# Packed loads, four warming products and a second issuing engine at the start of an attention, soft-MoE and gated-product kernel

## The chip, the cores and the metric

The kernel runs on one core of a Trainium2 chip. The metric is the device time of one execution in microseconds; lower is better. Of each run the profile gives, beside the time, the span from the first to the last instruction.

## What is computed

Three stages follow each other. Attention: 4 batches of 12 heads, 448 tokens of 64 numbers each, float32. Queries and keys are divided by their root mean square and multiplied by gains, then come the scaled scores, the softmax and the product with the values. Its output, laid out as 1792 tokens of 768 numbers, goes through a soft mixture of experts (8 experts of 4 slots, hidden width 1024), and that through a gated product.

```python
q_n, k_n = rmsnorm(q, g_q), rmsnorm(k, g_k)
scores = q_n @ k_n.T / sqrt(64)
attn = softmax(scores)
x = (attn @ v) as [1792, 768]
...
logits = x @ phi                      # 768 x 32
slots = softmax(logits, over tokens).T @ x
slot_out[e] = relu(slots[e] @ w1[e]) @ w2[e]
x = softmax(logits, over slots) @ slot_out
...
out = ((x @ w_a) * (x @ w_b)) @ w_out # 768 -> 1536 -> 768
```

## The kernel before

Attention works on 24 pairs of heads. A token row of 448 is cut into 4 chunks of 112 partitions (`NC`, `P`). For each pair `load_qk` brings queries and keys into one of three places in a wide tile (`xw` in the trace; pair p uses place p mod 3, so the load of pair 3 waits until pair 0 has been normalised, and that of pair 4 for pair 1). `square` and `sumsq` make the sums of squares (tiles `sq`, `ssq`), `rsqrt` the inverse roots (`nt`, `rinv`: a logarithm and an exponential on ScalarE, then three small steps on VectorE), `normalise` the normalised pair (tile `n`, one half on VectorE for the first two pairs, else all on GpSimd). `emit_T` transposes it on TensorE (`pst`) and writes four rounded parts into a tile `e`, of which there is one for all pairs but pair 1. `emit_Z` stacks these parts into the two tiles `z` of the pair by six transfers within the on-chip memory, three for each head: 64 rows of 1344, 448 and 896 numbers. All transfers are issued by SyncE, in program order.

The loop `for j in range(NPAIR + 1)` then goes through the pairs in 8 steps each. A step n issues `score(n+2)` (two products on TensorE into `pss`, and the row maximum `nmx` on VectorE), `expo(n+1)` (the exponential `p` on ScalarE, with the maximum as bias), `ptrans(n)` (the transpose of `p`, and its copy `pt`) and in every second step the products with the values. Preparing the pairs to come is spread over the steps: `emit_T` and `emit_Z` of pair j+2 in steps 4 to 6, the squares of pair j+4 on GpSimd in step 1, their sums on VectorE in steps 5 and 7.

Ahead of the loop stands a written-out start: `warm` (products of the identity matrix whose results nobody reads, 22 of them at first and `W1` = 15 just ahead of the first score), loads, `prep` (squares on ScalarE, sums on VectorE), `norm`, `normalise`, `emit_T` and `emit_Z` of pairs 0 and 1, then `prep` and `norm` of pairs 2 and 3, then `score(0)`, `score(1)` and `expo(0)`. The order on TensorE, ScalarE, GpSimd and SyncE is that of the code; on VectorE a scheduler fixes it when the program is built. Every engine works its own list in order, so that an instruction that waits holds up all behind it.

The two later stages stream the weights of the experts and of the gated product from HBM. The printed functions below are those that the change touches.

Of the kernel before, what the change touches and what calls it, by code (L numbers as in the profile page):

```python
# [32 lines left out]
def kernel(  # L33
    ctx: ExitStack,
    tc: tile.TileContext,
    q: bass.AP,
    k: bass.AP,
# [11 lines left out]
    B, H, S, D = q.shape  # L49
    NT, DM = out.shape  # L50
    E, F = w1.shape[0], 1024
    NS = phi.shape[1]
    DF = 128 * len(LAGS)
    NC = 4
    P = S // NC
# [27 lines left out]
    W1 = 15  # L83
# [107 lines left out]
    with ExitStack() as c1:  # L191
# [28 lines left out]
        def load_qk(p):  # L220
            if p >= NPAIR:
                return
            b, hp = divmod(p, HP)
            t = qk_sb[0:P, p % 3 * 1024:(p % 3 + 1) * 1024].rearrange("p (i h x) -> p i h x", i=2, h=2)
            for i, src in enumerate((q, k)):
                sp.dma_start(out=t[:, i], in_=src[b, 2 * hp:2 * hp + 2].rearrange("h (p c) d -> p h (c d)", c=NC))
            qk_t[p] = t

        def load_v(p):
            if p >= NPAIR:  # L230
                return
            b, hp = divmod(p, HP)
            src = v[b, 2 * hp:2 * hp + 2].rearrange("h (p c) d -> p h c d", c=NC)
            if p < NPAIR - 1:
                t = vp.tile([P, 2, NC, D], F32, tag="v", name=f"v{p}")
                sp.dma_start(out=t, in_=src)
                v_t[p] = [t[:, hd] for hd in range(2)]
            else:
                x = tk.tile([128, S], F32, tag="l4", name="v23a", bufs=1)[0:P, 0:NC * D]
                y = tk.tile([P, 4, 2, 32], F32, tag="c2", name="v23b", bufs=1)  # L240
                v_t[p] = x.rearrange("p (c d) -> p c d", d=D), y.rearrange("p c (a e) s -> p c (a e s)", a=2)
                for hd in range(2):
                    sp.dma_start(out=v_t[p][hd], in_=src[:, hd])
# [3 lines left out]
        def square(p, i, eng=None):  # L247
            if p >= NPAIR:
                return
            sq = sqp.tile([P, 512], F32, tag="sq", name="sq")  # L250
            a = qk_t[p][:, i].rearrange("p h x -> p (h x)")
            if eng is act:
                act.activation(out=sq, in_=a, func=AF.Square)
            else:
                pool.tensor_tensor(out=sq, in0=a, in1=a, op=ALU.mult)  # L255
            sq_t[p, i] = sq
# [38 lines left out]
        def normalise(p, eng=None):  # L295
# [3 lines left out]
            n_t[p] = npp.tile([P, 2, NC, 2, D], F32, tag="n", name=f"n{p}")  # L299
            for i in range(2):  # L300
                (eng if eng and i == 0 else pool).tensor_tensor(  # L301
                    out=n_t[p][:, i].rearrange("p c h d -> p h c d"),
                    in0=qk_t[p][:, i].rearrange("p h (c d) -> p h c d", d=D),
                    in1=rinv_t[p][:, i, :].rearrange("p (h c) -> p h c", h=2).unsqueeze(3).to_broadcast(
                        [P, 2, NC, D]
                    ),
                    op=ALU.mult,
# [3 lines left out]
        def emit_T(p, i):  # L311
# [12 lines left out]
            for c in range(NC):  # L324
                pe.transpose(ps[:, c * P:(c + 1) * P], src[:, i, c].rearrange("p h d -> p (h d)"), ident[0:P, 0:P])  # L325
# [10 lines left out]
        def emit_Z(p):  # L336
# [3 lines left out]
            for hd in range(2):  # L340
# [3 lines left out]
                sp.dma_start(out=z[D:128, 0].bitcast(F32), in_=src[:, 3])  # L344
# [214 lines left out]
        for i, g in enumerate((g_q, g_k)):  # L559
            for r in range(2):  # L560
                sp.dma_start(out=g4[r * D:(r + 1) * D, i:i + 1], in_=g.rearrange("(d o) -> d o", o=1))
        dve.scalar_tensor_tensor(
            out=gg, in0=g4[:, 0:1], scalar=float(D) ** 0.5, in1=g4[:, 1:2], op0=ALU.mult, op1=ALU.mult
        )
# [4 lines left out]
        norm(0)  # L569
        prep(1)  # L570
        normalise(0, dve)
# [6 lines left out]
        load_qk(4)  # L578
        prep(2)
        emit_T(1, 0)  # L580
        emit_T(1, 1)
        emit_Z(1)
        warm(ps_s.tile([128, 512], F32, tag="s", name="warm"), W1)
# [600 lines left out]
_INS = ["q", "k", "v", "g_q", "g_k", "moe_phi", "moe_w1", "moe_w2", "moe2_w"]  # L1184
# [38 lines left out]
```

## Time and profile before

| what | value |
|---|---|
| time, median of 3 runs | 591.48 us (590.6 to 592.62) |
| profiled execution | 593.33 us |
| its span | 591.5 us |
| PE busy | 557.4 us (94%) |
| ACT busy | 359.6 us (61%) |
| DVE busy | 349.6 us (59%) |
| mean granted TensorE clock | 0.984 |

The profile names PE for TensorE's products, PEld for its weight loads, DVE for VectorE, ACT for ScalarE, POOL for GpSimd and SPq for SyncE's queue of transfers. A shared time in the chain of work that ended last is the time in which that instruction, and nothing else, held up the end. The start, up to the first score, takes the first 21 us; the attention loop runs to some 340 us.

### The profile page before, as it was taken

To read this page: it belongs to the slowest core of one execution; us is meant where nothing else is said; L and a number is where in the kernel's file an instruction comes from. 1 tells how busy PE (TensorE), PEld (TensorE's weight loads), DVE (VectorE), ACT (ScalarE), POOL (GpSimd) and SP (SyncE) were. 2 spreads that over 40 slices of the span, in tenths; PEclk is the share of its full clock that TensorE was granted. 3 is DMA by queue.
4 is the path that set the end of the run, shared out by engine and by line. 5 is a ranking of instruction groups with operands and counts; after the bars stand their busy time and mean duration, and the time that the engine had idled before them with its cause. 6 is when DMAs were issued, how large, how long until landed. Compare 5 with 4: busy or idle time off the path is not lost.

```text
span 591.5 us, 10977 instructions
## 1 busy us (share of the span) xinstructions
PE 557.4 (94%) x3980; PEld 366.9 (62%) x3980; DVE 349.6 (59%) x703; ACT 359.6 (61%) x845; POOL 114.0 (19%) x136
## 2 busy tenths in 40 slices
PE   5989999999999999999999998898989999999997
PEld 5755555566565665655656554343665656689996
DVE  5877777678787687776767521122228888842210
ACT  4677787787887787877877721111169899432210
POOL 1233433333433333333110000010100000200000
PEclk9899999999999999999999999989989999999999
DMA  7955677788697978697676689999999993002332
GB/s 176 220 142 140 165 175 168 209 235 223 165 261 153 266 178 240 166 271 188 156 216 170 271 330 351 426 395 425 428 423 421 418 406 144 1 28 80 92 94 83
DMA packets 39573, 134.51 MB, mean 227 GB/s; under 512 B 5856, under 2 KB 25312, under 8 KB 33120
## 3 DMA queue, kind: packets, MB, share of 16 engines
q1 hardware_dynamic: 39520, 133.81, 72.0%
q8 instruction: 32, 0.52, 0.4%
q14 instruction: 21, 0.17, 0.1%
HBM read 95.26 MB, written 5.51 MB: 170 GB/s over the span
## 4 chain that ended last, share of the span: by engine, by line
PE 75%; DMA 10%; DVE 4%; ACT 4%; SPq 3%; issue 2%; ACTq 0%; DVEq 0%
PE psv L396 12%; PE pspt L382 11%; PE pss L358 5%; DMA z<-e 5%; PE pss L359 5%; PE psM L938 5%; DMA wu_w<-in_moe_w_dram 5%; PE pso L1138 3%; PE pso L1140 3%; PE pso L1139 3%; PE psS L721 3%; PE psh L697 3%; PE pst L325 3%; PE psS L938 2%; PE psx L509 2%
## 5 line engine op out<-in xcount | busy, mean ns | idle before, releaser
L360 DVE TENSOR_REDUCE nmx<-pss 112x1 f32<-112x448 f32 x192 | 118.4, 619 | 40.9 <-PE pss L359 40.5
L369 ACT ACTIVATE p<-pss,nmx 112x448 f32<-112x448 f32 x192 | 123.7, 644 | 9.2 <-DVE nmx L360 6.3
L382 PEld LDWEIGHTS pspt<-ident,p 112*112 112x112 f32 x768 | 80.4, 133 | 78.9 <-ACT pt L388 27.5
L382 PE MATMUL pspt<-ident,p 112*112 112x112 f32 x768 | 110.0, 266 | 1.5 <-ACT p L369 1.4
L388 ACT COPY pt<-pspt 112x448 f32<-112x448 f32 x144 | 76.9, 534 | 27.1 <-PE pspt L382 25.6
L396 PE MATMUL psv<-pt,v 112*64 112x448 f32 x368 | 90.3, 569 | 0.0
L358 PE MATMUL pss<-z 128*112 128x448 f32 x192 | 85.1, 443 | 0.0
L301 POOL TENSOR_TENSOR n<-xw,rinv 112x512 f32<-112x512 f32 x46 | 47.1, 1043 | 174.7 <-PE pst L325 109.7
L359 PE MATMUL pss<-z 128*112 128x448 f32 x192 | 70.5, 367 | 0.0
L386 DVE COPY pt<-pspt 112x448 f32<-112x448 f32 x48 | 29.9, 623 | 20.9 <-PE pspt L382 20.8
L255 POOL TENSOR_TENSOR sq<-xw 112x512 f32<-112x512 f32 x40 | 40.9, 1041 | 5.4 <-DMA xw<-in_q_dram 4.9
L369 ACT ACTIVATION_READ_ACCUMULATOR p<-pss,nmx 112x1 f32 x192 | 40.0, 208 | 0.0
L1138 PE MATMUL pso<-Mh,t 128*128 128x384 f32 x112 | 37.9, 338 | 0.5 <-DVE Ml L967 0.5
L358 PEld LDWEIGHTS pss<-z 128*112 128x112 f32 x192 | 34.0, 177 | 6.7 <-issue 5.8
L1139 PE MATMUL pso<-Ml,t 128*128 128x384 f32 x112 | 37.7, 337 | 0.0
L1140 PE MATMUL pso<-Mh,t 128*128 128x384 f32 x112 | 37.7, 337 | 0.0
L325 PE MATMUL pst<-ident,n 112*128 112x112 f32 x192 | 27.1, 267 | 10.9 <-ACT rd L427 6.3
L1157 DVE COPY ot<-pso 128x384 f32<-128x384 f32 (+1 forms) x14 | 7.6, 543 | 49.5 <-PE pso L1142 49.5
L396 PEld LDWEIGHTS psv<-pt,v 112*64 112x64 f32 x368 | 18.3, 135 | 29.5 <-issue 22.4
L359 PEld LDWEIGHTS pss<-z 128*112 128x112 f32 x192 | 34.2, 178 | 0.7 <-issue 0.6
L938 PE MATMUL psM<-w,G 128*128 128x512 f32 x64 | 33.8, 610 | 0.8 <-DVE w L818 0.8
L818 DVE SCALAR_TENSOR_TENSOR xw<-wu_w,top 128x768 int32<-128x768 int32 x24 | 22.3, 953 | 19.6 <-ACT top L804 19.6
(177 smaller groups left out, 891.7 us busy)
## 6 DMA issues: line engine op xcount, KB each, us to landing
wu_w<-in_moe_w_dram SPq DMA_DIRECT2D x38, 1536.0 KB, 11.0
z<-e SPq DMA_DIRECT2D x48, 336.0 KB, 4.6
z<-e SPq DMA_DIRECT2D x48, 224.0 KB, 4.4
r<-in_moe_w_dram SPq DMA_DIRECT2D x7, 1536.0 KB, 8.6
xw<-in_moe_w_dram SPq DMA_DIRECT2D x4, 1536.0 KB, 13.7
xw<-in_q_dram SPq DMA_DIRECT2D x24, 224.0 KB, 4.5
xw<-in_k_dram SPq DMA_DIRECT2D x24, 224.0 KB, 4.0
z<-e SPq DMA_DIRECT2D x48, 112.0 KB, 4.4
```

The source lines that it names most:

```text
L301: (eng if eng and i == 0 else pool).tensor_tensor(out=n_t[p][:, i].rearrange("p c h d -> p h c d"), in0=qk_t[p][:, i].rearrange("p h (c d) ...
L358: pe.matmul(ps, x, z[:, 1, :], start=True, stop=False)
L359: pe.matmul(ps, x, z[:, 2, :], start=False, stop=True)
L360: dve.tensor_reduce(out=nm_of[n // 8][:, h % 2, c:c + 1], in_=ps, axis=AX.X, op=ALU.max, negate=True)
L369: act.activation(out=t, in_=ps_of.pop(n), func=AF.Exp, bias=nm_of[n // 8][:, h % 2, c:c + 1], accum_out=den_t[n // 8][:, h % 2, c:c + 1],)
L382: pe.transpose(ps[:, kc * P:(kc + 1) * P], src[:, kc * P:(kc + 1) * P], ident[0:P, 0:P])
L388: act.copy(out=o, in_=i)
L396: pe.matmul(av_t[p][hd * D:(hd + 1) * D, 0:S], v_t[p][hd][:, kc, :], pt_t[2 * p + hd][:, kc, :], start=(kc == 0), stop=(kc == NC - 1),)
L938: pe.matmul(o, G[:, r], W[:, c], start=st, stop=sp_)
L1138: pe.matmul(o, ch[:, m], Mh[:, m, c], start=(m == 0), stop=False)
L1139: pe.matmul(o, ch[:, m], Ml[:, m, c], start=False, stop=False)
L1140: pe.matmul(o, cl[:, m], Mh[:, m, c], start=False, stop=False)
```

## The change

Queries and keys are packed on the host into one array `qk`, whose rows hold both, in the order in which they are normalised, and the values are laid out likewise; one transfer now loads a pair (two for pair 0). `W1` is 4 instead of 15. The middle one of the three transfers of each stack (64 rows of 448) is issued by ScalarE for pairs 0 and 1. `normalise(0)` stands ahead of `prep(1)`, the product of the gains (tile `few`) behind both, and `load_qk(4)` and `prep(2)` behind `emit_Z(1)`.

```diff
--- before.py
+++ after.py
@@ -33,8 +33,7 @@
 def tile_attention_softmoe_gate_kernel(
     ctx: ExitStack,
     tc: tile.TileContext,
-    q: bass.AP,
-    k: bass.AP,
+    qk: bass.AP,
     v: bass.AP,
     g_q: bass.AP,
     g_k: bass.AP,
@@ -46,13 +45,16 @@
 ):
     nc = tc.nc
     pe, act, dve, pool, sp = nc.tensor, nc.scalar, nc.vector, nc.gpsimd, nc.sync
-    B, H, S, D = q.shape
     NT, DM = out.shape
+    D = g_q.shape[0]
+    NC = 4
+    P = qk.shape[1]
+    S = NC * P
+    B = NT // S
+    H = DM // D
     E, F = w1.shape[0], 1024
     NS = phi.shape[1]
     DF = 128 * len(LAGS)
-    NC = 4
-    P = S // NC
     HP = H // 2
     NPAIR = B * HP
     KD = DM // 128
@@ -80,7 +82,7 @@
     W3 = 2
     W4 = 7
     W5 = 3
-    W1 = 15
+    W1 = 4
     DV = 7
     P2_ENGINES = {ET.PE, ET.SP}
 
@@ -220,27 +222,26 @@
         def load_qk(p):
             if p >= NPAIR:
                 return
-            b, hp = divmod(p, HP)
-            t = qk_sb[0:P, p % 3 * 1024:(p % 3 + 1) * 1024].rearrange("p (i h x) -> p i h x", i=2, h=2)
-            for i, src in enumerate((q, k)):
-                sp.dma_start(out=t[:, i], in_=src[b, 2 * hp:2 * hp + 2].rearrange("h (p c) d -> p h (c d)", c=NC))
-            qk_t[p] = t
+            qk_t[p] = qk_sb[0:P, p % 3 * 1024:(p % 3 + 1) * 1024].rearrange("p (i x) -> p i x", i=2)
+            if p == 0:
+                for i in range(2):
+                    sp.dma_start(out=qk_t[p][:, i], in_=qk[p][:, i])
+            else:
+                sp.dma_start(out=qk_t[p], in_=qk[p])
 
         def load_v(p):
             if p >= NPAIR:
                 return
-            b, hp = divmod(p, HP)
-            src = v[b, 2 * hp:2 * hp + 2].rearrange("h (p c) d -> p h c d", c=NC)
             if p < NPAIR - 1:
                 t = vp.tile([P, 2, NC, D], F32, tag="v", name=f"v{p}")
-                sp.dma_start(out=t, in_=src)
+                sp.dma_start(out=t, in_=v[p])
                 v_t[p] = [t[:, hd] for hd in range(2)]
             else:
                 x = tk.tile([128, S], F32, tag="l4", name="v23a", bufs=1)[0:P, 0:NC * D]
                 y = tk.tile([P, 4, 2, 32], F32, tag="c2", name="v23b", bufs=1)
                 v_t[p] = x.rearrange("p (c d) -> p c d", d=D), y.rearrange("p c (a e) s -> p c (a e s)", a=2)
                 for hd in range(2):
-                    sp.dma_start(out=v_t[p][hd], in_=src[:, hd])
+                    sp.dma_start(out=v_t[p][hd], in_=v[p][:, hd])
 
         sq_t = {}
 
@@ -248,7 +249,7 @@
             if p >= NPAIR:
                 return
             sq = sqp.tile([P, 512], F32, tag="sq", name="sq")
-            a = qk_t[p][:, i].rearrange("p h x -> p (h x)")
+            a = qk_t[p][:, i]
             if eng is act:
                 act.activation(out=sq, in_=a, func=AF.Square)
             else:
@@ -296,15 +297,11 @@
             if p >= NPAIR:
                 return
             assert not any(x[0] == p for x in small)
-            n_t[p] = npp.tile([P, 2, NC, 2, D], F32, tag="n", name=f"n{p}")
+            n_t[p] = npp.tile([P, 2, 8, D], F32, tag="n", name=f"n{p}")
             for i in range(2):
                 (eng if eng and i == 0 else pool).tensor_tensor(
-                    out=n_t[p][:, i].rearrange("p c h d -> p h c d"),
-                    in0=qk_t[p][:, i].rearrange("p h (c d) -> p h c d", d=D),
-                    in1=rinv_t[p][:, i, :].rearrange("p (h c) -> p h c", h=2).unsqueeze(3).to_broadcast(
-                        [P, 2, NC, D]
-                    ),
-                    op=ALU.mult,
+                    out=n_t[p][:, i], in0=qk_t[p][:, i].rearrange("p (n d) -> p n d", d=D),
+                    in1=rinv_t[p][:, i].unsqueeze(2).to_broadcast([P, 8, D]), op=ALU.mult,
                 )
             qk_t.pop(p)
 
@@ -322,7 +319,7 @@
             src = n_t[p]
             ps = ps_m.tile([128, 512], F32, tag="m", name="pst")[:, 0:S]
             for c in range(NC):
-                pe.transpose(ps[:, c * P:(c + 1) * P], src[:, i, c].rearrange("p h d -> p (h d)"), ident[0:P, 0:P])
+                pe.transpose(ps[:, c * P:(c + 1) * P], src[:, i, 2 * c:2 * c + 2].rearrange("p h d -> p (h d)"), ident[0:P, 0:P])
             if i == 0:
                 act.activation(out=et[:, 0], in_=ps, func=AF.Copy)
                 dve.tensor_tensor(out=et[:, 3], in0=ps, in1=et[:, 0].bitcast(F32), op=ALU.subtract)
@@ -341,7 +338,7 @@
                 z = zt[(2 * p + hd) % NZ]
                 src = et[hd * D:(hd + 1) * D].bitcast(F32)
                 sp.dma_start(out=z[0:D, 0:3].bitcast(F32), in_=src[:, 0:3])
-                sp.dma_start(out=z[D:128, 0].bitcast(F32), in_=src[:, 3])
+                (act if p < 2 else sp).dma_start(out=z[D:128, 0].bitcast(F32), in_=src[:, 3])
                 sp.dma_start(out=z[D:128, 1:3].bitcast(F32), in_=src[:, 1:3])
 
         def score(n):
@@ -559,27 +556,27 @@
         for i, g in enumerate((g_q, g_k)):
             for r in range(2):
                 sp.dma_start(out=g4[r * D:(r + 1) * D, i:i + 1], in_=g.rearrange("(d o) -> d o", o=1))
-        dve.scalar_tensor_tensor(
-            out=gg, in0=g4[:, 0:1], scalar=float(D) ** 0.5, in1=g4[:, 1:2], op0=ALU.mult, op1=ALU.mult
-        )
         load_qk(2)
         load_v(0)
         sp.dma_start(out=phi_sb, in_=phi.rearrange("(k p) s -> p k s", p=128))
         prep(0)
         norm(0)
+        normalise(0, dve)
+        dve.scalar_tensor_tensor(
+            out=gg, in0=g4[:, 0:1], scalar=float(D) ** 0.5, in1=g4[:, 1:2], op0=ALU.mult, op1=ALU.mult
+        )
         prep(1)
-        normalise(0, dve)
         load_qk(3)
         emit_T(0, 0)
         emit_T(0, 1)
         emit_Z(0)
         norm(1)
         normalise(1, dve)
-        load_qk(4)
-        prep(2)
         emit_T(1, 0)
         emit_T(1, 1)
         emit_Z(1)
+        load_qk(4)
+        prep(2)
         warm(ps_s.tile([128, 512], F32, tag="s", name="warm"), W1)
         norm(2)
         normalise(2)
@@ -1181,7 +1178,7 @@
             split(i + 2)
 
 
-_INS = ["q", "k", "v", "g_q", "g_k", "moe_phi", "moe_w1", "moe_w2", "moe2_w"]
+_INS = ["qk", "v", "g_q", "g_k", "moe_phi", "moe_w1", "moe_w2", "moe2_w"]
 _OUTS = [((1792, 768), "float32")]
 
 
@@ -1205,6 +1202,12 @@
 
     nc = _bacc.Bacc("TRN2", target_bir_lowering=False, num_devices=1)
     arrays, args = {}, []
+    q, k, v = (inputs.pop(x) for x in "qkv")
+    b, h, n, d = q.shape
+    q, k, v = (x.reshape(b, h // 2, 2, n // 4, 4, d) for x in (q, k, v))
+    qk = _np.stack([x.transpose(0, 1, 3, 4, 2, 5) for x in (q, k)], axis=3)
+    inputs["qk"] = qk.reshape(b * h // 2, n // 4, 2, 8 * d)
+    inputs["v"] = v.transpose(0, 1, 3, 2, 4, 5).reshape(b * h // 2, n // 4, 2, 4, d)
     inputs["moe2_w"] = _in_units(*(inputs.pop(f"moe2_w_{x}") for x in ("a", "b", "out")))
     for name in ("moe_w1", "moe_w2"):
         a = inputs[name]
```

The change moves instructions on three engines, all in the start.

ScalarE's list from the first copy of pair 0's transpose on, before (`e_208` and `z_141`, `z_142` are pair 0, `e_248` pair 1; `ssq_198`, `ssq_243`, `ssq_297` are pairs 1, 2 and 3; `p_319` is the first exponential):

```order
L327 ACTIVATE e_208<-pst 128x448
L330 ACTIVATE e_208<-pst,few 128x448
L286 ACTIVATE nt<-ssq_198,few 112x16
L287 ACTIVATE rinv_229<-nt 112x16
L253 ACTIVATE sq<-xw_65 112x512 x2
L327 ACTIVATE e_248<-pst 128x448
L330 ACTIVATE e_248<-pst,few 128x448
L286 ACTIVATE nt<-ssq_243,few 112x16
L287 ACTIVATE rinv_285<-nt 112x16
L253 ACTIVATE sq<-xw_65 112x512 x2
L286 ACTIVATE nt<-ssq_297,few 112x16
L369 ACTIVATE p_319,den<-pss,nmx 112x448
```

ScalarE's list from pair 0's second copy on, in the change (`e_205`, `e_236` are pairs 0 and 1, `ssq_199`, `ssq_260`, `ssq_282` pairs 1, 2 and 3, `p_304` the first exponential):

```order
L327 ACTIVATE e_205<-pst,few 128x448
L341 DMA z_141<-e_205 64x448
L341 DMA z_142<-e_205 64x448
L287 ACTIVATE nt<-ssq_199,few 112x16
L324 ACTIVATE e_236<-pst 128x448
L327 ACTIVATE e_236<-pst,few 128x448
L341 DMA z_143<-e_236 64x448
L341 DMA z_144<-e_236 64x448
L254 ACTIVATE sq<-xw_65 112x512 x2
L287 ACTIVATE nt<-ssq_260,few 112x16
L254 ACTIVATE sq<-xw_65 112x512 x2
L366 ACTIVATE p_304,den<-pss,nmx 112x448
```

Two issues of transfers now stand behind each pair's copies, and the two squares of pair 2 stand behind pair 1's instead of ahead of them.

VectorE's list from the last parts of pair 1 to the fifth row maximum, before (`ssq_412` are the sums of pair 4):

```order
L331 SCALAR_TENSOR_TENSOR e_248<-pst,few,e_248 128x448
L288 SCALAR_TENSOR_TENSOR nt<-rinv_285 112x16
L290 SCALAR_TENSOR_TENSOR nt<-ssq_243,nt 112x16
L263 TENSOR_REDUCE ssq_297<-sq 112x8
...
L292 SCALAR_TENSOR_TENSOR rinv_302<-nt,rinv_302 112x16
L360 TENSOR_REDUCE nmx<-pss 112x1 x3
L263 TENSOR_REDUCE ssq_412<-sq 112x8 x2
L360 TENSOR_REDUCE nmx<-pss 112x1
L386 COPY pt_329<-pspt 112x4x112
L360 TENSOR_REDUCE nmx<-pss 112x1 x4
```

The same stretch of VectorE's list in the change (`ssq_396` are the sums of pair 4):

```order
L328 SCALAR_TENSOR_TENSOR e_236<-pst,few,e_236 128x448
L357 TENSOR_REDUCE nmx<-pss 112x1
L264 TENSOR_REDUCE ssq_260<-sq 112x8 x2
L357 TENSOR_REDUCE nmx<-pss 112x1 x2
...
L293 SCALAR_TENSOR_TENSOR rinv_287<-nt,rinv_287 112x16
L264 TENSOR_REDUCE ssq_396<-sq 112x8
L357 TENSOR_REDUCE nmx<-pss 112x1
L383 COPY pt_313<-pspt 112x4x112
L264 TENSOR_REDUCE ssq_396<-sq 112x8
L357 TENSOR_REDUCE nmx<-pss 112x1 x4
```

The sums of pair 2 have moved behind the first maximum, and a sum of pair 4 stands ahead of the fourth maximum as before, the other now between the fourth and the fifth.

SyncE's list between the load of pair 3 and that of pair 4, before (the load of pair 4 is the two rows of `in_q_dram` and `in_k_dram`):

```order
L345 DMA z_142<-e_208 64x896
L226 DMA xw_65<-in_q_dram 112x2x256
L226 DMA xw_65<-in_k_dram 112x2x256
L343 DMA z_143<-e_248 64x1344
L344 DMA z_143<-e_248 64x448
L345 DMA z_143<-e_248 64x896
```

SyncE's list between the same loads in the change (the last row is the loads of pairs 4 and 5):

```order
L230 DMA xw_65<-in_qk_dram 112x1024
L340 DMA z_141<-e_205 64x1344
L342 DMA z_141<-e_205 64x896
L340 DMA z_142<-e_205 64x1344
L342 DMA z_142<-e_205 64x896
L340 DMA z_143<-e_236 64x1344
L342 DMA z_143<-e_236 64x896
L340 DMA z_144<-e_236 64x1344
L342 DMA z_144<-e_236 64x896
L230 DMA xw_65<-in_qk_dram 112x1024 x2
```

The load of pair 4 stood between the stacks of pairs 0 and 1 and now stands behind both. From there on, and on TensorE and GpSimd apart from the eleven products, the lists are the same but for the packed loads.

## Rows read from the trace of the kernel before

**Rows 1.** Busy time by stretch, with granted clock, DMA share and GB/s.

```profile
21.00:61.00 40.00, 36.46 (x227) 22.70 (x225) 30.66 (x62) 30.60 (x84) 14.63 (x16) 0.96 0.67 155
61.00:340.00 279.00, 271.83 (x1795) 165.38 (x1794) 203.69 (x439) 218.13 (x594) 82.97 (x91) 1.00 0.77 204
395.00:475.00 80.00, 73.12 (x641) 45.12 (x644) 39.52 (x57) 44.02 (x52) 4.83 (x5) 0.96 1.01 421
```

**Rows 2.** The chain that ended last, in order of time: start, us, what.

```profile
16.79 0.68 DVE e L331
...
20.85 0.99 DVE nt L290
...
22.04 1.59 DVE nmx L360 x3
23.64 1.19 DVE ssq L263 x2
24.82 0.54 DVE nmx L360
...
36.94 4.42 DMA z<-e
```

**Rows 3.** Timeline of the start: start, us, engine, instruction, idle before it.

```profile
8.18 0.68 DVE L301 TENSOR_TENSOR n<-xw,rinv 112x512 f32<-112x512 f32 x1
...
10.52 0.31 ACT L286 ACTIVATE nt<-ssq,few 112x16 f32<-112x16 f32 x1
10.68 0.68 DVE L331 SCALAR_TENSOR_TENSOR e<-pst,few,e 128x448 fp32r<-128x448 f32 x1
...
12.62 1.04 POOL L301 TENSOR_TENSOR n<-xw,rinv 112x512 f32<-112x512 f32 x1 [4.38 <-DVE rinv L292]
12.91 1.30 DVE L301 TENSOR_TENSOR n<-xw,rinv 112x512 f32<-112x512 f32 x1
...
14.36 1.72 PE L325 MATMUL pst<-ident,n 112*128 112x112 f32 x8 [4.45 <-DVE n L301]
```

**Rows 4.** Timeline of SyncE's queue: transfers issued.

```profile
11.94 0.59 SPq L344 DMA_DIRECT2D z<-e  x1
...
14.37 1.02 SPq L344 DMA_DIRECT2D z<-e  x1
...
17.72 0.66 SPq L226 DMA_DIRECT2D xw<-in_k_dram  x1
...
32.92 0.47 SPq L343 DMA_DIRECT2D z<-e  x1
```

**Rows 5.** Transfers issued at 17.5 to 18 us: KB, us to landing.

```profile
xw<-in_k_dram SPq DMA_DIRECT2D x1, 224.0 KB, 4.1
```

**Rows 6.** Timeline from the warming products to the loop.

```profile
15.87 5.39 PE L186 MATMUL warm<-ident 128*128 128x128 f32 x30
...
20.76 1.04 POOL L255 TENSOR_TENSOR sq<-xw 112x512 f32<-112x512 f32 x1
...
21.02 0.44 PE L358 MATMUL pss<-z 128*112 128x448 f32 x1
...
22.61 0.64 ACT L369 ACTIVATE p<-pss,nmx 112x448 f32<-112x448 f32 x1 [2.85 <-DVE nmx L360]
...
25.47 0.64 ACT L369 ACTIVATE p<-pss,nmx 112x448 f32<-112x448 f32 x1 [0.29 <-DVE nmx L360]
...
26.51 0.65 ACT L369 ACTIVATE p<-pss,nmx 112x448 f32<-112x448 f32 x1
```

**Rows 7.** Busy time by stretch: the stack of pair 2, and a later stretch.

```profile
34.00:40.50 6.50, 6.50 (x46) 4.14 (x44) 4.43 (x10) 4.02 (x13) 1.24 (x2) 1.00 0.96 213
43.00:47.00 4.00, 4.00 (x17) 1.93 (x16) 2.51 (x6) 2.51 (x8) 2.04 (x2) 0.58 0.28 58
```

**Rows 8.** DMA view, 395 to 470 us: the streamed weights.

```profile
DMA packets 2906, 31.77 MB, mean 424 GB/s; under 512 B 322, under 2 KB 322, under 8 KB 322
```

**Rows 9.** Timeline of ScalarE around pair 3's first copy.

```profile
41.61 0.54 ACT L327 ACTIVATE e<-pst 128x448 fp32r<-128x448 f32 x1 [2.79 <-DMA z<-e]
```

## Prediction, made before the changed kernel ran

> **What bounds the kernel now.** I read the busy time by stretch first. From 61 to 340 us TensorE is busy 271.83 of 279 us, from 395 to 475 us the transfers are busy all the time, at 421 GB/s [rows 1]. Neither stretch is touched by the change but for the packed loads, so what the change is worth is read from the first 61 us, and then it is asked whether a shift there reaches the end. From 21 to 61 us TensorE is idle 3.5 us, and its busy time there includes waits at a lower clock.
>
> Second, the chain that ended last, from 16 to 42 us. The reader is to see that it does not run through the warming products. It goes through the last part of pair 1 (ends 17.47), sums of squares and two small steps of the inverse root on VectorE that are drawn out to about 1 us, the first three row maxima at 22.04, the sums of pair 4 (1.19 us), the fourth maximum at 24.82, then ScalarE's exponentials, and the stack of pair 2 [rows 2]. The warming products end at 21.26 and the first score starts at 21.02, so they release the scores less than 1 us ahead of the moment at which VectorE would have come to a maximum anyway [rows 2, 6]. So the start has two chains of nearly one length: TensorE's, which the change shortens, and that of preparing pairs 2 to 4, whose order it changes.
>
> Third, the timelines of the start for the durations, and SyncE's queue for the order of the transfers.
>
> **The change, part by part.**
>
> *Four products instead of 15.* Fifteen took 5.39 us, 0.36 each; eleven fewer are 3.95 us of TensorE [rows 6]. Beside the other chain this alone is worth at most the few tenths between the third score and the first maximum.
>
> *Pair 0.* VectorE's list now has both sums of pair 1 and the gains ahead of the last step of pair 0's root or of `normalise`. Half of the normalising is VectorE's, and beside GpSimd's half (12.62 to 13.66) it took 1.30 us in pair 1, against 0.68 in pair 0 [rows 3]. I take it that VectorE's half now ends behind GpSimd's, 0.4 us later than before (bounds 0 and 0.9; the packed first load, of which the trace has no row, may give some of it back). The last part of pair 0 then ends at 11.36 + 0.4 = 11.8.
>
> *ScalarE issues transfers.* No row of before shows ScalarE issuing. The nearest are SyncE's issues of the same transfer, 0.59 and 1.02 us [rows 4]; the bounds are 0 and 1.0 each, and I take 0.6. Behind the two issues wait the logarithm of pair 1 (10.52 before), and with it everything of pair 1: it starts at about 11.25 + 1.2 = 12.5. From the logarithm to pair 1's transposes took 10.52 to 14.36, 3.84 us, with two sums of pair 2 in VectorE's way (about 0.65 each), which are now behind; 2.5 us remain, so the transposes start at about 15.0, 0.6 later, less up to 0.6 if the normalising no longer waits for GpSimd. Pair 1's last part ends at 17.7 (16.5 with free issues, 18.7 with dear ones) against 17.47.
>
> *Squares of pair 2 behind pair 1.* Before, they were done while pair 1 waited. Now two issues (1.2), the two squares, two sums, logarithm and exponential, two squares of pair 3, its two sums, and again logarithm and exponential stand between pair 1's copy (ends 17.0) and the first exponential of the loop: about 7 us. It starts at 24.0 against 22.61 [rows 6]. So the eleven products give TensorE only a longer idle stretch.
>
> *The load of pair 4 behind the second stack.* This is the term that I take to decide. Before, it stood ahead of pair 1's stack and landed at 17.72 + 4.1 = 21.8 [rows 4, 5]; GpSimd squared its first half at 20.76 [rows 6]. On VectorE the fourth maximum stands behind the sum of that square, before as after. Now both stacks are ahead of it in SyncE's queue. One stack, undisturbed, lands 8.4 us after its first issue (32.92 to 36.94 + 4.42) [rows 2, 4]. Its 1344 KB (1.38 MB) go at 213 GB/s, 6.5 us, with the transfer engines busy 0.96 of that time [rows 7]. Pair 0's stack is issued at 11.8 and lands at 20.2; pair 1's, issued at 17.7 while the first still runs, follows 6.5 us later, at 26.7; the load of 448 KB (0.46 MB) adds 1.1 us even at the 424 GB/s of the weights [rows 8]: 27.8. ScalarE's transfers go out a little ahead, so I take **27.5**. Bounds: if two queues let the stacks overlap fully, only issuing limits, and the load lands some 24.4; with dear issues and the load at the stack's rate, 29.
>
> The Trainium skill, "DMA: Bandwidth & Descriptors", section "Issuing engines are not separate DMA queues", says that transfers from different issuing engines run on the same 16 DMA engines and that a second issuer only saves issue time. By that rule the bound of 24.4 is out of reach and the time would be the one from 27.8; no run of before has a second issuer.
>
> *From the load to the loop.* Square 1.04, sum 0.6, hand-overs 0.1: the fourth maximum starts at 29.2 against 24.82, and the exponential that waited for it (25.47, idle until that maximum) at 29.9, 4.4 later. The second sum of pair 4 now stands between the fourth and fifth maximum, 0.6 more: the next exponential (26.51) comes **5.0 us later** [rows 2, 6]. This covers the 1.4 us of the first exponential.
>
> *TensorE's clock.* After an idle stretch of about 2 us the granted clock was 0.58 from 43 to 47 us [rows 7], between the levels of 1.2 and 2.4 GHz. Now TensorE idles longer, from its third score on. A repeat would cost up to 1.7 us (4 us at 0.58 do the work of 2.3). In the first pair of the loop ScalarE paces, which hides some of it: I take 0, and keep 1.7 for the upper end.
>
> *Packed loads later on.* They save an issue for each of 21 further pairs and some transfer time. Both lie beside a TensorE that is busy 97%, and behind the stack in the queue. I take 0; at most 2 us, a part of the 7.2 us of TensorE's idle time between 61 and 340 us. If a load were waited for, that would show as a gain there.
>
> *Does the shift reach the end?* The loop's first pair ends in pair 2's stack, for which ScalarE waited 2.79 us [rows 9]; the wait moves along, since the stack does. From there TensorE is nearly full, and the weights stream into places which attention frees. Nothing absorbs it.
>
> **Sum.** 0 for the products, 5.0 for the load of pair 4, 0 for clock and later loads. The profiled execution had a span of 591.50 and 1.83 us around it; with 5.0 it would have 596.5 and 598.3. The median of the runs, 591.48, stands at that span, so I forecast **596.5 us**.
>
> **The rivals.**
>
> *Faster: the products were the bound.* If pair 4's load lands by 22.9 and the first exponential comes ahead of 22.6, the loop follows the earlier scores and gains up to 3.95 us: 587.5. For it speaks that the first score started as the products ended [rows 6]. Against it: the first exponential stands behind both roots on ScalarE, and the load behind 2.7 MB of stacks. It decides at whether the stacks move much above 213 GB/s when two engines issue.
>
> *The same: issues are nearly free and the stacks overlap.* Pair 1 is then ready at 16.5 and the load lands at some 23.5; GpSimd ends pair 2's halves at 23.8, so the square ends at 24.9, the fourth maximum starts at 25.6 to 26.1, and the fifth is 1.4 late: 592.9. Against it: the transfer engines were already busy 0.96 with one issuer [rows 7].
>
> *Slower still: the clock.* The load as in the sum, and TensorE at the lower level where the loop begins: 598.2.
>
> *The change does not do what it says:* the packed loads shorten nothing that is waited for. That is already in the sum.
>
> **How the numbers follow.** The forecast's own range is 593.4 (landing at 24.4) to 599.7 (29, and the clock). I give it 0.70, the clock as a case of its own within it 0.06, no change 0.11, faster 0.13. The range runs from 590.8, half of the case without change, to 599.5. A measurement of this kernel can tell about 0.3%, 1.8 us. Slower by more: 0.76; within: 0.11; faster: 0.13.
>
> **What would show it.** Right: the square of pair 4 on GpSimd waits for a load until about 27.5; the fourth maximum waits behind its sum; ScalarE idles ahead of the fourth exponential until about 29.9; the first exponential starts at about 24; pair 2's stack is issued at about 38 instead of 32.92; the stretch from 61 to 340 moves unchanged. Wrong: if that load lands by 24, if the two sets of issues on ScalarE take next to nothing, or if TensorE's idle time behind 61 us shrinks by more than 2 us.

## The result, and the profile after

| | median | lowest to highest | profiled execution, its span |
|---|---|---|---|
| before (6 runs, 3 of them new) | 590.75 us | 590.09 to 592.62 | 593.33 us, 591.5 us |
| changed (6 runs) | 596.23 us | 594.61 to 598.65 | 595.62 us, 593.7 us |

The ratio is 1.0088, 95% interval 1.0061 to 1.0116: the change makes the kernel slower by 5.2 us at the 591 us of before (3.6 to 6.9). The forecast was 596.5 us. The two profiled executions lie only 2.3 us apart, since that of before stood above its own median; sizes below come from ratios, places and orders from the traces.

The timeline of the start in the changed kernel (start, us, engine, line, instruction, idle before it):

```profile
8.78 0.16 DVE L565 SCALAR_TENSOR_TENSOR few<-few 128x1 f32<-128x1 f32 x1 [1.81 <-DMA few<-in_g_k_dram]
...
11.43 0.98 PE L322 MATMUL pst<-ident,n 112*128 112x112 f32 x8 [2.82 <-DVE n L302]
...
13.30 1.16 ACTq L341 DMA_DIRECT2D z<-e  x2
...
14.50 0.31 ACT L287 ACTIVATE nt<-ssq,few 112x16 f32<-112x16 f32 x1 [1.36 <-DVE e L328]
...
19.81 0.72 PE L355 MATMUL pss<-z 128*112 128x448 f32 x1
...
23.48 3.93 SPq L230 DMA_DIRECT2D xw<-in_qk_dram  x2
...
25.94 0.62 ACT L366 ACTIVATE p<-pss,nmx 112x448 f32<-112x448 f32 x1
...
28.63 2.04 POOL L256 TENSOR_TENSOR sq<-xw 112x512 f32<-112x512 f32 x2 [1.57 <-DMA xw<-in_qk_dram]
29.70 0.69 DVE L264 TENSOR_REDUCE ssq<-sq 112x8 f32<-112x512 f32 x1 [2.19 <-POOL sq L256]
30.30 0.61 DVE L357 TENSOR_REDUCE nmx<-pss 112x1 f32<-112x448 f32 x1
31.03 0.63 ACT L366 ACTIVATE p<-pss,nmx 112x448 f32<-112x448 f32 x1 [2.14 <-DVE nmx L357]
...
31.96 1.15 DVE L357 TENSOR_REDUCE nmx<-pss 112x1 f32<-112x448 f32 x2
...
32.67 0.64 ACT L366 ACTIVATE p<-pss,nmx 112x448 f32<-112x448 f32 x1 [0.49 <-DVE nmx L357]
...
39.08 0.47 SPq L340 DMA_DIRECT2D z<-e  x1
```

Read against [rows 3, 4, 6]: the first score came 1.2 us earlier (19.81 for 21.02), and the first exponential all the same 3.3 us later (25.94 for 22.61). The fourth exponential waits for the chain that the prediction named: load of pair 4, square on GpSimd, sum, fourth maximum. It came 5.6 us later (31.03 for 25.47), the fifth 6.2 (32.67 for 26.51), the stack of pair 2 6.2 (39.08 for 32.92). New, and in no term of the prediction, is the first row: VectorE stood 1.81 us waiting for the gains, and all of pair 0 behind it.

The chain of waits of the changed kernel (start, us, what) holds both the wait for the gains and that for the load:

```profile
4.01 4.65 DMA few<-in_g_k_dram
...
23.48 5.02 DMA xw<-in_qk_dram
28.54 0.09 issue
28.63 1.05 POOL sq L256
29.70 0.69 DVE ssq L264
30.39 0.53 DVE nmx L357
```

The busy time by stretch of the changed kernel; 21 to 61 us and the rest of the loop answer to [rows 1], the last two are 3 us each:

```profile
21.00:61.00 40.00, 32.88 (x184) 21.10 (x185) 28.61 (x60) 27.94 (x78) 13.34 (x14) 0.85 0.62 157
61.00:340.00 279.00, 273.55 (x1804) 166.21 (x1800) 207.11 (x446) 220.22 (x600) 85.89 (x93) 1.00 0.75 200
...
22.00:25.00 3.00, 0.40 (x2) 0.00 (x0) 2.97 (x9) 1.56 (x4) 0.00 (x0) 0.88 1.01 247
...
28.00:31.00 3.00, 3.00 (x14) 2.39 (x12) 1.30 (x3) 0.89 (x3) 2.04 (x2) 0.50 0.47 153
```

Between 21 and 61 us TensorE was busy 3.6 us less (32.88 for 36.46) and its clock fell from 0.96 to 0.85; from 28 to 31 us it ran at 0.50, the lower level (1.2 GHz), after an idle stretch (0.40 us busy of the 3 from 22 to 25). From 61 to 340 us the clock is 1.00 as before.

Not all of the shift reaches the end of attention. ScalarE's wait for the stack of pair 4, and the last exponential of the loop, before (first) and changed (second):

```profile
67.92 0.54 ACT L327 ACTIVATE e<-pst 128x448 fp32r<-128x448 f32 x1 [1.94 <-DMA z<-e]
...
336.45 0.63 ACT L369 ACTIVATE p<-pss,nmx 112x448 f32<-112x448 f32 x1 [0.38 <-ACT p L369]
```

```profile
72.73 0.54 ACT L324 ACTIVATE e<-pst 128x448 fp32r<-128x448 f32 x1 [0.76 <-DMA z<-e]
...
340.90 0.63 ACT L366 ACTIVATE p<-pss,nmx 112x448 f32<-112x448 f32 x1 [0.38 <-ACT p L366]
```

The shift is 6.2 us at the fifth exponential, 4.8 behind this copy (72.73 for 67.92) and 4.5 at the last exponential (340.90 for 336.45); 1.2 us of it goes where ScalarE waits 0.76 us for the stack and not 1.94.

### The profile page after: what moved, and what is told of

Same layout as the page of the kernel before. It is cut to its first block, busy times and chain, and to the rows that moved or that the text cites. A ratio compares the mean times of both kernels' runs of the same rounds, so it can differ in the third digit from the quotient of the medians.

```text
span 593.7 us, 10872 instructions
## 1 busy us (share of the span) xinstructions
PE 555.8 (94%) x3958; PEld 365.6 (62%) x3958; DVE 348.4 (59%) x703; ACT 360.7 (61%) x845; POOL 114.4 (19%) x136
## 4 chain that ended last, share of the span: by engine, by line
PE 72%; DMA 16%; ACT 4%; DVE 3%; SPq 3%; issue 2%; ACTq 0%; POOL 0%; DVEq 0%; POOLq 0%
PE psv L393 12%; PE pspt L379 11%; DMA wu_w<-in_moe_w_dram 9%; PE pss L355 6%; DMA z<-e 5%; PE pss L356 5%; PE psM L935 4%; PE pso L1135 3%; PE pso L1136 3%; PE pso L1137 3%; PE pst L322 3%; PE psS L718 3%; PE psh L694 2%; PE psS L935 2%; PE psx L506 2%
## 5 line engine op out<-in xcount | busy, mean ns | idle before, releaser
L379 PEld LDWEIGHTS pspt<-ident,p 112*112 112x112 f32 x768 | 81.6, 135 | 83.2 <-ACT pt L385 27.5
L379 PE MATMUL pspt<-ident,p 112*112 112x112 f32 x768 | 111.6, 268 | 5.3 <-ACT p L366 5.1
L355 PE MATMUL pss<-z 128*112 128x448 f32 x192 | 86.8, 452 | 0.0
L356 PE MATMUL pss<-z 128*112 128x448 f32 x192 | 71.8, 374 | 0.0
L355 PEld LDWEIGHTS pss<-z 128*112 128x112 f32 x192 | 34.9, 182 | 6.8 <-issue 6.5
L356 PEld LDWEIGHTS pss<-z 128*112 128x112 f32 x192 | 35.1, 183 | 0.7 <-issue 0.6
L264 DVE TENSOR_REDUCE ssq<-sq 112x8 f32<-112x512 f32 x48 | 32.4, 677 | 4.9 <-ACT sq L254 2.7
```

The source lines that it names most:

```text
L355: pe.matmul(ps, x, z[:, 1, :], start=True, stop=False)
L356: pe.matmul(ps, x, z[:, 2, :], start=False, stop=True)
L379: pe.transpose(ps[:, kc * P:(kc + 1) * P], src[:, kc * P:(kc + 1) * P], ident[0:P, 0:P])
```

## The experiments

Every ratio is to the kernel before, run on the same chip. There the kernel before took 591.6 to 592.8 us, more than the 590.75 above, so differences below come from ratios and not from raw times. Half the interval of a ratio is 0.002 to 0.0035, so a difference of two is uncertain by about 2 us (root of 0.0028² and 0.0021², times 591). Where a step of the code moves, the scheduler may also give VectorE another order; it is told where it matters.

**The load of pair 4 ahead again.**

```diff
         normalise(1, dve)
+        load_qk(4)
         emit_T(1, 0)
         emit_T(1, 1)
         emit_Z(1)
-        load_qk(4)
         prep(2)
```

> The changed kernel with one edit undone: the load of pair 4 again ahead of the stack of pair 1; the lists of ScalarE, VectorE, GpSimd and TensorE are the same as in the changed kernel. Theory of the prediction (the load of pair 4, queued behind both stacks, decides alone): the fourth maximum starts about 3.6 us earlier than the 30.30 us of the changed kernel and the time falls by about 3.6, to 592.6. Rival (the whole start is late, because VectorE waits for the gains and ScalarE's list is longer, and the load only tops it): GpSimd ends pair 2's halves at 27.06, so the square of pair 4 ends at 28.1 instead of 29.7 and no more than 1.5 us come back: 594.7. Rival (the load is hidden): no change, 596.2.

Measured: 593.87 us, ratio 1.0035 [1.0014, 1.0055]; against 1.0088 that is 3.1 us better. The timeline of this kernel:

```profile
23.99 2.04 POOL L302 TENSOR_TENSOR n<-xw,rinv 112x512 f32<-112x512 f32 x2 [7.66 <-DVE rinv L293]
...
25.99 2.04 POOL L256 TENSOR_TENSOR sq<-xw 112x512 f32<-112x512 f32 x2
...
28.57 0.61 DVE L357 TENSOR_REDUCE nmx<-pss 112x1 f32<-112x448 f32 x1
```

The square of pair 4 no longer waits for its load; it starts right behind pair 2's normalising. By the medians the order of the load was worth some 3 us, not 5: one link behind it stands another that is nearly as late, pair 2's inverse root, which the next runs take up. In this execution, though, the gains came in time and pair 0's transposes started 1.0 us earlier (10.40 for 11.43), so of the 1.7 us by which the fourth maximum is ahead (28.57 for 30.30) only some 0.7 are left for the order. The 3.1 us stand on the medians alone.

**The product of the gains on GpSimd**, so that VectorE can't wait for them.

```diff
-        dve.scalar_tensor_tensor(
-            out=gg, in0=g4[:, 0:1], scalar=float(D) ** 0.5, in1=g4[:, 1:2], op0=ALU.mult, op1=ALU.mult
-        )
+        pool.tensor_tensor(out=gg, in0=g4[:, 0:1], in1=g4[:, 1:2], op=ALU.mult)
+        pool.tensor_scalar(out=gg, in0=gg, scalar1=float(D) ** 0.5, scalar2=None, op0=ALU.mult)
```

> The changed kernel with the product of the gains made by GpSimd behind its half of pair 0, instead of by VectorE ahead of pair 0's root. Theory (the wait of 1.81 us for the gains' load on VectorE shifts everything behind it): pair 0's transposes start at 9.2 to 9.6 instead of 11.43, the square of pair 4 waits for its load until 26.3 to 26.8 instead of 28.54, and the time falls by about 2, to 594.2. Rival (the stacks and the load set the pace from the queue, and the early part is hidden): under 0.5 us come back, 595.8 or more.

Measured: 593.78 us, 1.0040 [1.0011, 1.0069], 2.8 us better. The timeline of this kernel:

```profile
9.18 0.99 PE L322 MATMUL pst<-ident,n 112*128 112x112 f32 x8 [1.15 <-DVE n L302]
...
26.73 2.04 POOL L256 TENSOR_TENSOR sq<-xw 112x512 f32<-112x512 f32 x2 [2.12 <-DMA xw<-in_qk_dram]
...
28.41 0.61 DVE L357 TENSOR_REDUCE nmx<-pss 112x1 f32<-112x448 f32 x1
```

Pair 0's transposes start at 9.18 (8.92 before), 2.25 us ahead of the changed kernel's, and the fourth maximum 1.89 ahead (28.41 for 30.30): a late pair 0 delays the stacks, and with them the load behind them.

**Both together**, the two edits above in one kernel.

> The changed kernel with both edits: gains on GpSimd, load of pair 4 ahead of the stack of pair 1. If the late start and the late load are two terms that add up, 3.5 us come back, 592.7, and the fourth maximum starts at about 26.8. If the load alone decides, as much as with that edit alone. If something else in the start decides (the two squares of pair 2 behind pair 1 on ScalarE), the first exponential stays at 24 or later and less than 2.5 us come back, 593.7 or more.

Measured: 591.35 us, 0.9997 [0.9976, 1.0018]. Within the intervals the two add up (0.0053 and 0.0048 alone, 0.0091 together), and the loss is gone, but so is what the four products might bring.

**Both, and the squares of pair 2 ahead of pair 1's copies, as they were.**

```diff
         load_qk(4)
+        prep(2)
         emit_T(1, 0)
         emit_T(1, 1)
         emit_Z(1)
-        prep(2)
```

> The changed kernel with the gains on GpSimd and with the load and the squares of pair 4 and 2 again ahead of pair 1's transposes. Theory (what is left to the kernel before is the first exponential, which stands behind pair 2's squares): the first exponential starts at 20 to 21.5 instead of 23.55, the fourth at 24 to 25.5 instead of 27.12, and the time is 589 to 590.5. Rival (the stacks set the pace, or VectorE's small steps beside GpSimd): 591 or more, as with gains and load alone (591.35).

Measured: 589.20 us, 0.9943 [0.9917, 0.9970], 3.2 us better than with the squares behind. The timeline: first exponential, fourth maximum and fifth exponential, for 23.55, 26.40 and 28.76 with the squares behind:

```profile
22.06 0.62 ACT L366 ACTIVATE p<-pss,nmx 112x448 f32<-112x448 f32 x1
...
24.15 0.62 DVE L357 TENSOR_REDUCE nmx<-pss 112x1 f32<-112x448 f32 x1 [0.64 <-PE pss L356]
...
26.82 0.64 ACT L366 ACTIVATE p<-pss,nmx 112x448 f32<-112x448 f32 x1
```

The fourth maximum now waits for the score, no longer for VectorE's and GpSimd's work on pairs 2 to 4. Against the kernel before, the fifth exponential is still 0.3 us late (26.82 for 26.51), the last one 2.1 early (334.40 for 336.45): what this kernel gains over the one before does not lie at the start of its loop. 1.2 us of it are ScalarE's wait for the stack of pair 4, 0.74 for 1.94 us.

**Four products alone, in the order of before.**

```diff
-    W1 = 15
+    W1 = 4
```

> The kernel before with four warming products instead of 15 and nothing else; the scheduler then sets the first three maxima on VectorE ahead of the small steps of pair 3's root. Theory of the prediction (the products stand beside a second chain of nearly one length): no more than a few tenths come, 591.0 to 591.6. Rival (with VectorE's new order the second chain gets shorter too): the first exponential starts at about 20 instead of 22.61, the fourth at 23.5 to 24.5 instead of 25.47, and the time is 589.5 to 590.5. Rival (TensorE falls to its lower level without the products): granted clock under 0.7 between 22 and 28 us and 592 or more.

Measured: 589.05 us, 0.9938 [0.9908, 0.9968]: 3.7 us (1.9 to 5.4) faster than before, where the prediction had a few tenths. The timeline of this kernel:

```profile
17.45 0.72 PE L358 MATMUL pss<-z 128*112 128x448 f32 x1
...
19.01 1.68 DVE L360 TENSOR_REDUCE nmx<-pss 112x1 f32<-112x448 f32 x3
...
22.80 0.61 DVE L360 TENSOR_REDUCE nmx<-pss 112x1 f32<-112x448 f32 x1
...
25.15 0.63 ACT L369 ACTIVATE p<-pss,nmx 112x448 f32<-112x448 f32 x1 [0.48 <-DVE nmx L360]
```

The first score starts 3.6 us earlier than in [rows 6]. The first three maxima go ahead of pair 3's root on VectorE, an order that the scheduler chose with the products gone, so the second chain of the start shortens as well. Of the 3.6 us less than half gets through: the fifth exponential is 1.4 us early (25.15 for 26.51), the last one 1.5 (334.92 for 336.45); between them, behind the stack of pair 4, it is 2.6. The rest of the 3.7 us shows in no row of the attention; the interval reaches down to 1.9.

The step of 1.2 us at the stack of pair 4 goes with the count of products. In the nine traces with four of them ScalarE waits 0.72 to 0.77 us there, in the five with ten or fifteen 1.74 to 2.03. In the kernel before, a packet of 16 KB of an instruction queue is moved while that stack is under way, at 65.1 us (the view of the transfers from 64.9 to 66.1 us: queue, packets, MB, share):

```profile
q8 instruction: 1, 0.02, 4.9%
```

In the five traces it starts 2.6 to 3.2 us ahead of ScalarE's copy, in the nine at most 0.2 us ahead of it. So the fewer products may have moved a transfer of code out of the stack's way; no run tests this alone.

**Fifteen products in the changed kernel.**

```diff
-    W1 = 4
+    W1 = 15
```

> The changed kernel with fifteen products in place of four, all else as it is. It tells whether the products were worth anything inside the change. Theory (the prediction's term of 0: inside the change the scores wait for the load of pair 4, so eleven products more are hidden, and a clock that stays up may give back a little): 595.0 to 597.0 us by the kernel before at 591, ratio 1.006 to 1.010, the fourth maximum within 0.5 us of its 30.30. Rival (the products are worth the same 3.6 us as in the order of before): 599 or more, ratio 1.014 or more.

Measured: 597.85 us, 1.0107 [1.0073, 1.0142]: 1.1 us behind the changed kernel, less than the two intervals tell apart. The timeline:

```profile
22.29 2.35 SPq L230 DMA_DIRECT2D xw<-in_qk_dram  x2
...
25.63 0.62 DVE L357 TENSOR_REDUCE nmx<-pss 112x1 f32<-112x448 f32 x1 [0.29 <-PE pss L356]
...
28.94 2.04 POOL L256 TENSOR_TENSOR sq<-xw 112x512 f32<-112x512 f32 x2 [4.64 <-DMA xw<-in_qk_dram]
...
31.15 0.61 DVE L357 TENSOR_REDUCE nmx<-pss 112x1 f32<-112x448 f32 x1
```

Inside the change eleven products more cost nothing that can be told, as the prediction said. The expectation on the fourth maximum was missed, since the scheduler gave VectorE another order: the fourth maximum now stands ahead of the sum of pair 4 and starts 4.7 us earlier (25.63 for 30.30), and it is the fifth that waits for the load's chain (31.15, in the changed kernel 31.96). Pair 0 was 1.2 us early here, yet pair 4's load is squared 6.65 us after its issue, not 5.15. Two things differ: VectorE has pair 2's root ahead of the maxima, pair 2 is normalised at 24.3 and not at 27.1, so that the load of pair 5 may start and is issued right behind that of pair 4; and the last transfer of the stacks took 6.2 us to landing, not 5.0. Which of the two held the load up is not separated.

**All stack transfers issued by SyncE**, the change otherwise as it is.

```diff
-                (act if p < 2 else sp).dma_start(out=z[D:128, 0].bitcast(F32), in_=src[:, 3])
+                sp.dma_start(out=z[D:128, 0].bitcast(F32), in_=src[:, 3])
```

> The changed kernel with all transfers of the stacks issued by SyncE. The scheduler then sets VectorE's list a little differently: the fourth maximum stands ahead of the first sum of pair 4, the fifth behind it. Theory (the stacks run at the rate of the transfer engines, whoever issues): the landing of pair 4's load stays within 1 us of 28.5, and the time is 595.5 to 596.7; the 1.2 us for which ScalarE issues are covered by the queue. Rival (ScalarE's issues are on the path): 1.2 us or more come back, 595.0 or less. Rival (the second issuer speeds the stacks): the load lands 1 us later or more, 597 or more.

Measured: 597.82 us, 1.0100 [1.0068, 1.0132], not told apart from the changed kernel. The timeline:

```profile
13.11 0.50 SPq L340 DMA_DIRECT2D z<-e  x1
...
23.17 1.39 SPq L342 DMA_DIRECT2D z<-e  x1
...
24.66 1.44 SPq L230 DMA_DIRECT2D xw<-in_qk_dram  x2
...
30.55 2.04 POOL L256 TENSOR_TENSOR sq<-xw 112x512 f32<-112x512 f32 x2 [5.92 <-DMA xw<-in_qk_dram]
```

From the first issue of a stack to the square of pair 4 it took 17.4 us, with two issuers 15.3 (13.30 to 28.63). The last transfer of the stacks, issued at 23.17 here and at 22.14 there, landed after the time in the last column, here (first row) and in the changed kernel (second):

```profile
z<-e SPq DMA_DIRECT2D x1, 224.0 KB, 4.6
```

```profile
z<-e SPq DMA_DIRECT2D x1, 224.0 KB, 5.0
```

So both stacks took 14.7 us (13.11 to 27.8) with one issuer and 13.8 (13.30 to 27.1) with two: 0.9 us less, not a rate of another order. The other 1.2 us lie between the landing of the stacks and the square. Here, too, VectorE was ahead with pair 2's root, and the load of pair 5 went out with that of pair 4 ("x2", within 1.44 us; in the changed kernel over 3.93); that this is the reason is argued, not shown. The run thus bears out that a second issuer lets the load land earlier, but not that it speeds the stacks much.

**ScalarE's issues alone, on top of four products in the order of before.**

```diff
-                sp.dma_start(out=z[D:128, 0].bitcast(F32), in_=src[:, 3])
+                (act if p < 2 else sp).dma_start(out=z[D:128, 0].bitcast(F32), in_=src[:, 3])
```

> Before with four products, and the middle stack transfer of the first two pairs issued by ScalarE; the load of pair 4 stands where it stood, between the stacks. Theory (a second issuer shortens the stacks by 1 to 2 us, but costs ScalarE 1.1 us per issue ahead of pair 1's operations): the first score product 0 to 1 us earlier, the time 588.0 to 590.0, no change that can be told from 589.05. Rival (the shorter stacks come through): 588 or less. Rival on the other side (pair 1 is 1.2 us later and holds all behind it): 590.2 or more.

Measured: 591.38 us, 0.9969 [0.9942, 0.9996], 1.8 us behind the four products alone, within what the intervals leave open. The trace says how it would come: pair 1's logarithm starts at 11.80 for 10.50, behind two issues (1.14 us for both, not for each); the first exponential at 22.12 for 19.66, since VectorE's maxima now stand between the sums of pair 3.

**Packed loads alone, in the order of before** (the loads, squares and the normalising of the diff, `W1` = 15, SyncE for all stacks). Its core:

```diff
-            for i, src in enumerate((q, k)):
-                sp.dma_start(out=t[:, i], in_=src[b, 2 * hp:2 * hp + 2].rearrange("h (p c) d -> p h (c d)", c=NC))
...
+                sp.dma_start(out=qk_t[p], in_=qk[p])
```

> The kernel before with the packed loads and nothing else; the scheduler then sets the gains on VectorE ahead of the last steps of pair 0's root. Theory (the gains' wait comes with the packed loads by way of VectorE's list): pair 0's transposes start 1 to 2.5 us later than 8.92 and the time is 592.5 to 594. Rival (packed loads land sooner and that shows): 590.5 or less. Rival (they change nothing): 591.5.

Measured: 593.87 us, 1.0019 [0.9994, 1.0044], not told apart from no change. The gains are late here too:

```profile
8.54 0.16 DVE L559 SCALAR_TENSOR_TENSOR few<-few 128x1 f32<-128x1 f32 x1 [1.14 <-DMA few<-in_g_k_dram]
```

**Packed loads with four products and the gains on GpSimd**, to see the loads without that wait: the kernel with packed loads, and

```diff
-    W1 = 15
+    W1 = 4
...
-        dve.scalar_tensor_tensor(
+        pool.tensor_tensor(out=gg, in0=g4[:, 0:1], in1=g4[:, 1:2], op=ALU.mult)
+        pool.tensor_scalar(out=gg, in0=gg, scalar1=float(D) ** 0.5, scalar2=None, op0=ALU.mult)
```

> Before with four products, the packed loads and the product of the gains on GpSimd, all stack transfers by SyncE. It stands against the kernel before with four products alone (589.05 us, ratio 0.9938). Theory (the packed loads bring nothing by themselves; all that they did was to hold up VectorE by the late gains): the first pst at 9.2 us or a little later, the time within 1 us of 589.0, 588.2 to 590. Rival (the packed loads help once the gains are out of the way): the fourth maximum ahead of 22.2 us and the time under 588.0.

Measured: 589.95 us, 0.9950 [0.9920, 0.9980], for 0.9938 without packing. The packed loads gave nothing that can be told, nor cost it, once VectorE doesn't wait for the gains.

**Fifteen products, with load and gains put right, and ten with the squares too**: what the clock is worth.

```diff
-    W1 = 4
+    W1 = 15
```

```diff
-    W1 = 4
+    W1 = 10
```

> The kernel with gains on GpSimd and the load of pair 4 ahead of pair 1's stack, with 15 warming products again. Theory (TensorE's low level at the start of the loop costs 1 to 1.7 us): the granted clock stays over 0.9 from 22 to 31 us and the time falls from 591.35 to 590. Rival (ScalarE and VectorE set the pace there and the clock is hidden): 591 to 591.7. Rival (the products now hold up the scores): 592 or more.

> The changed kernel with the load of pair 4 and the squares of pair 2 where they were, the gains on GpSimd, and ten products in place of four. It stands against the same with four (589.20 us, ratio 0.9943). Theory (the granted clock falls to 0.5 for some us behind four products and costs about 1 us): the clock at 1.00 from 22 us on and the time 588.0 to 588.8. Rival (ten products hold up the scores by what the clock gives): 589.2 or more.

Measured: 590.68 us, 0.9969 [0.9940, 0.9999], for 0.9997 with four; and 589.07 us, 0.9929 [0.9906, 0.9952], for 0.9943 with four. Both ways more products are 0.8 to 1.7 us ahead, neither by more than the intervals leave open. The stretch from 25 to 28 us with gains, load and squares put right, four products (first) and ten (second):

```profile
25.00:28.00 3.00, 3.00 (x19) 2.43 (x17) 2.69 (x5) 2.28 (x7) 1.48 (x2) 0.70 0.59 172
```

```profile
25.00:28.00 3.00, 2.01 (x12) 1.23 (x12) 2.73 (x7) 2.88 (x9) 0.00 (x0) 1.00 0.50 142
```

In this pair the clock falls with four products (0.70 in these 3 us) and stays up with ten. But the count alone does not decide it. Four products alone in the order of before, 25 to 28 us (first), and the changed kernel with fifteen, 28 to 31 us (second):

```profile
25.00:28.00 3.00, 2.33 (x17) 1.61 (x16) 2.72 (x6) 2.83 (x9) 0.00 (x0) 1.00 1.04 239
```

```profile
28.00:31.00 3.00, 0.41 (x2) 0.00 (x0) 0.99 (x2) 0.23 (x1) 2.04 (x2) 0.50 0.10 29
```

The first keeps the full clock with four products, the second loses it with fifteen. The price of the lower clock stays at the 0.8 to 1.7 us of the two comparisons, by estimate, and is not shown.

By their intervals six versions are faster than the kernel before, among them four products alone (0.9938), the change with its three moves put right (0.9943), that with ten products (0.9929), and packed loads with four products and the gains on GpSimd (0.9950). These four can't be told apart. The other two have intervals that nearly reach 1: fifteen products with load and gains put right, and ScalarE's issues on top of four products (0.9969 each).

## Why the prediction was right, and which terms were not

The direction, the chain and the total were right; how the loss is shared among the moves was not, and that the total came so near (5.2 for 5.0 us) is in part luck. The sum had one term of 5.0 and zeros. Measured were three losses of about 3 us each and a gain of 3.7. The statement that nothing absorbs the shift did not hold in the trace: 6.2 us at the fifth exponential, 1.2 more than forecast, were 4.5 at the last.

- **The load of pair 4** was the term that decided, by its sum the whole 5.0 us. The chain stands as forecast: landing at 28.5 (27.5 forecast, bounds 24.4 to 29), fourth maximum 30.30 (29.2), fifth exponential 6.2 late (5.0), stack of pair 2 at 39.08 (about 38), 2.75 MB of stacks in 13.8 us, 199 GB/s, near the 213 of [rows 7]. But the order alone was worth 3.1 us by the medians, since the working asked only what this load would release, and not what comes next once it is on time.
- **Pair 0, "0.4 us later"**: mis-sized. It was 2.5 (11.43 for 8.92), and of it the normalising beside GpSimd, the part that was priced, is 0.48 (1.16 for 0.68 us). Most of the rest is the wait for the gains, 1.81. The prediction saw the product ahead of pair 0's root and gave what it waits for no term. Before, it stood at a place where VectorE had no need to wait. Worth 2.8 us in all. It is why pair 0's stack began at 13.3 and not at 11.8; with the gains on GpSimd the square of pair 4 started 1.9 us earlier (26.73 for 28.63), more than the 1.0 us by which the load came later than forecast.
- **The squares of pair 2** were priced rightly at the first exponential (1.4 us forecast; 23.55 with them behind and 22.06 with them ahead), and then taken as covered by the later load. With the load put right they cost 3.2 us.
- **The products, 0**: right inside the change, where fifteen were 1.1 us behind four, not told apart from nothing. As a statement on the kernel before it was wrong: there they were worth 3.7 us. The two chains of one length that the prediction read at 22 us were not independent: with four products the scheduler gives VectorE another order, and both became shorter.
- **Issues on ScalarE, 0.6 each**: right, 1.16 us for two in the trace, and pair 1's logarithm waited for them (14.50). **Packed loads, 0**: right for themselves, apart from the gains. **The clock, 0**: it did fall, to 0.50; 0.8 to 1.7 us by estimate, not shown.
- **The rivals.** That the stacks overlap fully fell: 13.8 us for both, for 14.7 with one issuer. The Trainium skill, "DMA: Bandwidth & Descriptors", section "Issuing engines are not separate DMA queues", has a second issuer save only issue time; these 0.9 us agree: without the second issuer SyncE came to the load behind the stacks 1.2 us later (24.66 for 23.48). The faster rival, in which the products are the bound, holds in part in the kernel before (3.7 of its 3.95 us by the medians, of which the trace shows 1.4 at the fifth exponential), but not in the change.

Ledger by ratios: four products alone −3.7; gains +2.8, load behind the stacks +3.1, squares behind pair 1 +3.2; sum +5.4, measured +5.2. They are differences taken in different orders, so the agreement is no proof of each; the three losses were taken back one after another (1.0088, 1.0035 or 1.0040, 0.9997, 0.9943), and that end is the four products' gain alone.

## What to carry to other kernels

When an instruction is moved forward in a list, price what it waits for at the new place, not only how long it takes: a product of 0.16 us cost 2.8, as the transfer that it waits for was late. When a moved step is late, ask what would hold the end if it were on time, since several moves can each cover the next; and test a small edit such as the count of products by itself, because here the whole gain lay in it and the three moves around it spent it and more.

## What the runs showed of the hardware that was not expected

A small load landed later, though it was issued earlier, when the large loads ahead of it were packed. The gains (0.2 KB) were issued 0.6 us earlier with the packed loads; why they landed later is not shown. The transfers issued from 2 to 5.2 us, before (first) and changed (second), the last column the us to landing:

```profile
few<-in_g_k_dram SPq DMA_DIRECT2D x2, 0.2 KB, 2.5
```

```profile
few<-in_g_k_dram SPq DMA_DIRECT2D x2, 0.2 KB, 4.5
```

It changes between traces: in five kernels with packed loads and the product of the gains on VectorE, VectorE waited for them 1.81, 1.14, 0.77, 0.60 us and once not at all. And pair 4's load took longer where pair 5's was issued right behind it: it was squared 5.89 and 6.65 us after its issue there, 5.15 and 5.59 where pair 5's came later (the changed kernel and that with the gains on GpSimd). The stacks ahead of it differ too, so sharing is argued, not shown.
